# A fused block-sparse attention and feed-forward kernel: probabilities of the late pairs transposed by DMA, late scores two pairs at a time, orders dealt anew

## The chip, the cores and the metric

The kernel runs on one core of a Trainium2 chip. The metric is the device time of one execution in microseconds (us). The kernel before takes 307.81 us, the median of three runs (306.92 to 307.94).

A core has TensorE (PE in the profile; weight loads are shown apart as PEld), VectorE (DVE), ScalarE (ACT), GpSimd (POOL), SyncE (SP) and 16 DMA engines. Each engine takes its instructions in program order and waits on semaphores. Here SP does nothing but issue DMAs and load registers for them.

## The reference

The attention has 4 batches, 8 heads, 768 positions and a head size of 64. Positions form 24 blocks of 32. A query block sees its two neighbours and itself, the first and the last block, and three sampled blocks; the first and the last query block see everything. Behind it stands a feed-forward network (FFN) with 512 inputs, 2048 hidden units and 512 outputs over all 3072 tokens.

```python
scores = scale * np.matmul(q, k.transpose(0, 1, 3, 2))
mask = np.abs(blk_i - blk_j) <= window
mask = mask | (blk_i == 0) | (blk_j == 0) | (blk_i == n_blocks - 1) | (blk_j == n_blocks - 1)
...
mask[qb * block:(qb + 1) * block, kb * block:(kb + 1) * block] = True
scores = np.where(mask, scores, -1000000000.0)
scores = scores - np.max(scores, axis=-1, keepdims=True)
attn = np.exp(scores)
attn = attn / (np.sum(attn, axis=-1, keepdims=True) + 1e-09)
return np.matmul(attn, v).astype(np.float32)
...
h = x @ w_in
g = h * (1.0 / (1.0 + np.exp(-beta * h)))
return (g @ w_out).astype(np.float32)
```

## The kernel before

**Attention by pairs.** The 22 inner query blocks of a batch are taken two at a time: 11 pairs per batch, 44 in all, numbered n = 0 to 43. Pairs 33 to 43 are those of the last batch. The steps of a pair are:

- `kg`, `kn` (L635, L638): POOL copies the sampled blocks of K into the tile KG, POOL or DVE the neighbouring ones.
- `vv`, `vg` (L664, L720): SP loads block numbers into registers and issues the DMAs that gather the V blocks from a table in DRAM (VT) into VG. An ordinary late pair has seven: six of 32 KB for the sampled blocks, one of 192 KB for the neighbours. VG has four slots.
- `sc` (L759, L769): PE writes the masks of a pair (8 matmuls) and its scores (16 matmuls) in tiles of 64 x 32 into two PSUM banks.
- `mx`, `ex` (L782, L790): DVE takes the maxima, ACT the exponentials into the tile PP (three buffers).
- `nrm` (L813, pairs from 11 on): POOL or DVE multiplies PP by the reciprocal sums.
- `tp` (L827): PE transposes the 128 x 1024 probabilities in eight matmuls of 128 x 128 into a PSUM bank. `ptv` (L832, seen as L313 on DVE and L311 on ACT) copies that bank to PT (two buffers).
- `av` (L854 from pair 16 on, 16 matmuls; L862 before): PE multiplies PT by VG. `xv` copies the result to xT.

The first and last query blocks of a batch go another way (`gs` L917 to `gav` L971), with their own exponentials `ge` (L938), six transposes `gt` (L957) and copies.

**The FFN** goes over the tokens in eight groups G of 8 or 16 blocks, as soon as their attention stands in xT: `h` (L1033, 64 matmuls for a group, 128 x 256 or 128 x 512), `tanh` on ACT (L1039), `stt` on DVE (L1044), `y` (L1060, 128 x 512 matmuls), `oe` on ACT (L1070, seen as L317), `od` on SP (L1078, L1080, L1081) to the output. The last group needs the last pairs.

**The order.** Every step is a task with engines, a planned cost and a priority. `Plan.run` (L65) deals the tasks out in a planned time and fixes each engine's order; on the chip each engine then follows that order blindly. `OFFSET` (L53) shifts priorities by name, `YIELD` (L51) those of tasks that have just become ready. `plan = Plan(8, 6)` (L304) lets the FFN hold six of eight PSUM banks while attention is left. `GATES` (L259) names the pairs whose V loads the loads of w_in and w_out wait for, `QV` (L260) how many halves of V must be ready before each half of the first Q load.

Of the kernel before, what the change touches and what calls it, by code (L numbers as in the profile page):

```python
# [37 lines left out]
class Plan:  # L38
# [12 lines left out]
    YIELD = 10  # L51

    OFFSET = {'tp': 6.0, 'av': -5, 'gs': -1.0, 'gt': 5, 'gav': 10, 'trK': 2.1, 'nrm': 5, 'ex': -10, 'ptv': 9.1, 'xv': 1.4, 'oe': 20, 'gm': 2, 'ge': 10, 'pick': -10, 'tp1': 5, 'ptv1': 15, 'mx1': 0.5, 'tp2': -21.2, 'av2': -5, 'kn2': 30, 'ptv2': 5, 'tp3': 60, 'kn3': -5, 'ptv3': -15, 'hl3': 14.4, 'kg4': -15, 'ex4': 0.6, 'tp5': 1.3, 'av5': 60, 'kn5': -5, 'ptv5': 12.3, 'kg7': 5, 'mx7': -10.0, 'tp9': 5, 'xv9': 30, 'av10': 15, 'kn10': -15, 'av11': 15, 'kn11': 0.5, 'hl12': 5, 'sc13': -0.6, 'ex13': -3.7, 'av14': -1.3, 'tp15': -3.4, 'kn15': 4.3, 'mx0.0': 60, 'mx1.0': -5, 'ex2.1': -5, 'ex4.1': -15, 'ex5.0': 15, 'ex5.1': -60, 'mx7.0': 5, 'mx7.1': 30, 'win': -0.5, 'oe2': -1.2, 'y3': -6.6, 'h4': -1.0, 'stt4': 15, 'h5': -0.2, 'h7': 5}  # L53
# [164 lines left out]
def kernel(  # L218
# [11 lines left out]
    nc = tc.nc  # L230
# [28 lines left out]
    GATES = (2, 2, 5)  # L259
    QV = (1, 2)  # L260
    NLATE, PTA, ODS, AHEAD = 11, 1.0, 0.8, 3
    NHOT, NV = 0, 2
    NHL, UP = 4, 1024.0
    WIDE = 16
# [35 lines left out]
    osb = [sb(f"osb{i}", [P, D_MODEL], FP32) for i in range(NO)]  # L300
    VT = [dram.tile([S, D_MODEL], FP16, name=f"VT{b}") for b in range(B)]
    banks = [psum.tile([P, 512], FP32, name=f"bank{i}") for i in range(8)]

    plan = Plan(8, 6)  # L304
# [86 lines left out]
    for part, f in enumerate((emit_mask0, emit_mask1, emit_mask2)):  # L391
# [7 lines left out]
        deps=[t_mb], prio=-66, closes=("mask",))  # L399

# [127 lines left out]
    trK, trQ, evK, evQ, vperm, vtab = {}, {}, {}, {}, {}, {}  # L528
    later = {b: [] for b in range(B)}
    for b in range(B):  # L530
# [24 lines left out]
        for nm, s16, dstT, tr, ev in (("K", RK, KT, trK, evK), ("Q", RQ, QT, trQ, evQ)):  # L555
            for hp in range(NHP):
# [37 lines left out]
        else:  # L594
            vtab[b] = [add(f"vtab{b}", "SP", 0.4, lambda b=b, vt_rows=vt_rows: nc.sync.dma_start(
                out=vt_rows, in_=Vn[b % 2]), deps=vperm[b], prio=pr + 5, dma=1.9, slack=1.0, hw=1)]
# [14 lines left out]
    xlate, picks = [], []  # L611
    held_n, vv, vv_of, vg_last = {}, None, None, None
# [4 lines left out]
    for n, (b, p) in enumerate(order_pairs):  # L617
# [11 lines left out]
        def emit_kg(b=b, p=p, kt32=kt32, kg32=kg32):  # L629
            _, vals = nc.values_load_multi_w_load_instructions(  # L630
                offP[0:1, p, 0:6], engines=(ET.Pool,), min_val=0, max_val=(NB - 1) * W,
                skip_runtime_bounds_check_because="block numbers lie below the number of blocks")
            for g in range(2):
# [34 lines left out]
        if n >= NSEL and (p % NV == 0 or n == NSEL):  # L668
            held_n[n] = min(NV - p % NV, NPAIR - p)
# [3 lines left out]
        elif n < NSEL:  # L673
            vv = None
# [5 lines left out]
        def moves(n=n, vgb=vgb, vt=vt, vt8=vt8, i0=i0, first=head_v, w0=6 * (n - vv_of) if n >= NSEL else 0):  # L680
# [19 lines left out]
            elif i0 + 1 < NB - 2:  # L700
                yield 0.6, lambda v: (
                    vgb[0:3 * BLK, :, 1, :],
                    bass.AP(tensor=vt.tensor, offset=vt.offset + (i0 - 1) * BLK * D_MODEL,
                            ap=[[D_MODEL, 3 * BLK], [BLK * D_MODEL, 2], [1, D_MODEL]]))
            else:
                yield 0.3, lambda v: (vgb[0:3 * BLK, 0, 1, :], vt[(i0 - 1) * BLK:(i0 + 2) * BLK, :])
                yield 0.1, lambda v: (vgb[0:BLK, 1, 1, :], vt[(NB - 1) * BLK:NB * BLK, :])
                yield 0.2, lambda v: (vgb[BLK:3 * BLK, 1, 1, :], vt[i0 * BLK:(i0 + 2) * BLK, :])
            for g in range(2 if n >= NSEL else 0):
                for r in range(3):  # L710
                    yield RND, lambda v, g=g, r=r: (
# [3 lines left out]
        for k_, (cost, f) in enumerate(moves()):  # L715
            def emit_vg(vv_of=vv_of if n >= NSEL else None, f=f):
                o, i = f(held.get(vv_of))
                if i.dtype != U8:
                    o, i = o.bitcast(U8), i.bitcast(U8)
                nc.sync.dma_start(out=o, in_=i)  # L720
            vg[n].append(add(f"vg{n}.{k_}", "SP", 0.5, emit_vg,
                             deps=[vv] + vtab[b] + ([av[vlast(n)]] if vlast(n) >= 0 else []) +
                             ([ld["Q", 0, hp] for hp in range(NHP)] if NVG <= n < 2 * NVG else []),
                             prio=vprio(n, k_), dma=cost, hw=1))
# [29 lines left out]
        def emit_sc(n=n, b=b, p=p, i0=i0, kgb=kgb):  # L754
            bk = [bank(("S", n, u)) for u in range(2)]
            ns = 5 if p in (0, NPAIR - 1) else 3
            for hp in range(NHP):
                for u in range(2):
# [6 lines left out]
                        tile_position=(u * D, hp * BLK))  # L765
            for g in range(2):
                for hp in range(NHP):
# [7 lines left out]
        sc[n] = add(f"sc{n}", "PE", 0.31, emit_sc,  # L775
                    deps=[kg[n], kn[n], t_mask] + [evQ[b, hp] for hp in range(NHP)], prio=pr, lat=0.2,
                    opens=(("S", n, 0), ("S", n, 1)))
# [43 lines left out]
        def emit_tp(n=n, pb=pb):  # L821
            o = bank16(("T", n))
            for g in range(2):
                for c in range(2):
                    for u in range(2):
                        s = (g * 2 + c) * 2 + u
                        nc.tensor.transpose(out=o[:, s * P:(s + 1) * P],  # L827
                                            in_=pb[:, u, g, c * P:(c + 1) * P], identity=identity)
        tp[n] = add(f"tp{n}", "PE", 0.45, emit_tp, deps=[nrm[n]] if nrm[n] else [ex[n, 0], ex[n, 1]], prio=pr - 0.5, lat=0.2,
                    opens=(("T", n),))  # L830
        ptv[n] = add(f"ptv{n}", {"DVE": 0.61, "ACT": PTA}, None, lambda eng, n=n: copy_on(
            eng, PT[n % NPT], bank16(("T", n))),  # L832
            deps=[tp[n]] + ([av[n - NPT]] if n >= NPT else []), prio=pr - 0.5, closes=(("T", n),))
# [3 lines left out]
        def emit_av(n=n, vgb=vgb, wide=wide, late=late, hl=HL[n % NHL]):  # L837
            o = bank(("O", n))
            pt = PT[n % NPT].rearrange("x (g c u m) -> x g c u m", g=2, c=2, u=2)
# [66 lines left out]
    for b in range(B):  # L906
        for w, (blk, u) in enumerate((bl, u) for bl in (NB - 1, 0) for u in range(2)):
# [28 lines left out]
            def emit_ge(m=m, s_=s_, pg=pg):  # L936
                for hf in range(2):
                    nc.scalar.activation(  # L938
                        out=pg[:, hf * (S // 2):(hf + 1) * (S // 2)], in_=bank(("GS", m, hf))[:, 0:S // 2],
# [13 lines left out]
            def emit_gt(m=m, pg=pg):  # L953
                o = bank16(("GT", m))
                pj = pg[:, :].rearrange("x (p j) -> x j p", j=J)
                for j in range(J):
                    nc.tensor.transpose(out=o[:, j * P:(j + 1) * P], in_=pj[:, j, :], identity=identity)  # L957
            gt[m] = add(f"gt{m}", "PE", 0.34, emit_gt, deps=[gn[m]], prio=pr, lat=0.2, opens=(("GT", m),))
# [38 lines left out]
    for b in range(2, B):  # L997
        old = [x[n] for n, (bb, _) in enumerate(order_pairs) if bb == b - 2 for x in (kg, kn)] + gsc_all[b - 2]
        oldq = [sc[n] for n, (bb, _) in enumerate(order_pairs) if bb == b - 2] + gsc_all[b - 2]
        for hp in range(NHP):  # L1000
            trK[b, hp].deps += old
            trQ[b, hp].deps += oldq
# [12 lines left out]
    for G, sz in enumerate(sizes):  # L1015
# [38 lines left out]
        for s in range(sz // 4):  # L1054
# [21 lines left out]
            def emit_od(ob=ob, base=base, row=row):  # L1076
                if row + P <= S:
                    nc.sync.dma_start(out=out[base + row:base + row + P, :], in_=ob)  # L1078
                else:
                    nc.sync.dma_start(out=out[base + row:base + S, :], in_=ob[0:S - row, :])  # L1080
                    nc.sync.dma_start(out=out[base:base + row + P - S, :], in_=ob[S - row:P, :])  # L1081
            out_dma.append(add(f"od{G}.{s}", "SP", 0.9 if row + P > S else 0.45, emit_od, deps=[te],
                               prio=at(0.5 + 2.0 * s / sz), slack=ODS, dma=0.7, hw=2 if row + P > S else 1))
# [36 lines left out]
```

## Time and profile before

| | |
|---|---|
| median of three runs | 307.81 us |
| profiled execution | 306.43 us |
| its span in the trace | 304.6 us |
| granted TensorE clock, mean | 0.987 |
| ACT busy / exponentials L790 | 219.7 us / 81.5 us |
| FFN matmuls L1033 + L1060 | 93.8 + 92.3 us |
| POOL normalizing L813 | 63.5 us |
| DVE copying transposed probabilities | 39 of 44 pairs, 685 ns each |
| ACT doing the same | 5 of 44 pairs, 1015 ns each |

An engine's busy time is the time covered by its instructions; matmuls overlap in a pipeline, so the mean of one matmul (224 ns for a 128 x 128 transpose) is far more than what it adds. The chain of waits is followed back from the last instruction, at each step to what released it. There a row such as "0.45 PE bank L827 x8" says that eight instructions of line 827 took 0.45 us of the chain.

### The profile page before, as it was taken

The page shows a single profiled execution, that of the slowest core. Times are in us where ns is not written, and L with a number is a line of the kernel's source. Part 1 is how long each engine was busy: PE and PEld are TensorE (multiplying, and loading weights), DVE is VectorE, ACT ScalarE, POOL GpSimd, SP SyncE. Part 2 cuts the span into 40 slices and gives each one's busy share as a digit, 9 for nine tenths or more (in the row PEclk, how much of TensorE's full clock was granted, in tenths as well). Part 3 has the DMA queues.
Part 4 walks back from the last instruction along what each step waited for, and adds up shares of the span by engine and source line. Part 5 has one row for each costly group of instructions (what it writes and reads, how often), then busy time and mean ns, then how long its engine had stood idle before and what let it go on. Part 6 is the DMA issues. An engine that isn't in the chain of part 4 may idle for free.

```text
span 304.6 us, 11650 instructions
## 1 busy us (share of the span) xinstructions
PE 285.8 (94%) x4209; PEld 178.0 (58%) x4209; DVE 242.3 (80%) x562; ACT 219.7 (72%) x639; POOL 172.7 (57%) x513
## 2 busy tenths in 40 slices
PE   1699799999999999999998999999999999999994
PEld 0455678658855785655556555556555555554671
DVE  4758989999999999999999579989789765780260
ACT  3347579889797998898758599977689837771461
POOL 3069995044689588899784386868646942100000
PEclk9999969999999999999999999999999999999999
DMA  7999999977999362479933643244332232101202
GB/s 248 369 293 200 236 234 233 222 211 138 175 189 193 109 192 76 132 144 178 201 116 117 204 132 97 70 131 135 113 119 67 68 119 90 37 0 58 82 1 69
DMA packets 43443, 44.15 MB, mean 145 GB/s; under 512 B 6005, under 2 KB 39414, under 8 KB 43386
## 3 DMA queue, kind: packets, MB, share of 16 engines
q1 hardware_dynamic: 31056, 32.13, 35.0%
q0 software_dynamic: 12320, 11.27, 24.0%
q8 instruction: 33, 0.54, 0.7%
q14 instruction: 24, 0.20, 0.2%
q10 hardware_dynamic: 10, 0.01, 0.0%
HBM read 45.23 MB, written 9.44 MB: 179 GB/s over the span
## 4 chain that ended last, share of the span: by engine, by line
PE 69%; DVE 17%; DMA 9%; ACT 2%; issue 1%; SPq 0%; POOL 0%; DVEq 0%
PE bank L1033 25%; PE bank L1060 20%; PE bank L827 5%; DMA VG<-VT 4%; DVE ST L782 4%; PE bank L854 3%; PE bank L561 3%; DVE SG L931 3%; DVE VG L313 3%; DMA g<-in_k_dram 3%; PE bank L735 3%; DMA g<-VT 2%; PE bank L759 2%; PE bank L769 2%; PE bank L862 2%; DVE PTG L959 2%
## 5 line engine op out<-in xcount | busy, mean ns | idle before, releaser
L790 ACT ACTIVATE PP<-bank,ST 128x256 f16<-128x256 f32 x176 | 81.5, 478 | 22.7 <-DVE ST L782 13.6
L1033 PE MATMUL bank<-xT,w_in_sb 128*128 128x256 f16 (+1 forms) x512 | 93.8, 327 | 1.6 <-DVE g L1044 0.9
L1060 PE MATMUL bank<-w_out_sb,g 128*128 128x512 f16 x384 | 92.3, 380 | 0.0
L1044 DVE SCALAR_TENSOR_TENSOR g<-t,bank 128x512 f16<-128x512 f16 (+1 forms) x128 | 66.6, 546 | 19.4 <-ACT t L1039 19.0
L1039 ACT ACTIVATE t<-bank,beta_sb 128x512 f16<-128x512 f32 (+1 forms) x128 | 70.3, 593 | 12.4 <-PE bank L1033 8.4
L813 POOL TENSOR_SCALAR PP<-PP,ST 128x256 f16<-128x256 f16 x132 | 63.5, 499 | 27.6 <-DVE ST L807 27.0
L635 POOL COPY KG<-KT 128x64 f32 x264 | 51.8, 247 | 31.9 <-PE bank L769 18.9
L1033 PEld LDWEIGHTS <-w_in_sb 128*128 128x128 f16 x512 | 53.7, 114 | 26.1 <-issue 4.6
L782 DVE TENSOR_REDUCE ST<-bank 128x2 f32<-128x512 f32 x88 | 57.4, 681 | 3.4 <-PE bank L769 2.2
L1060 PEld LDWEIGHTS <-g 128*128 128x128 f16 x384 | 34.4, 98 | 38.2 <-issue 4.9
L790 ACT ACTIVATION_READ_ACCUMULATOR PP<-bank,ST 128x1 f32 x176 | 36.6, 208 | 0.0
L317 ACT ACTIVATE osb<-bank 128x512 f32<-128x512 f32 x24 | 14.5, 606 | 19.6 <-PE bank L1060 19.4
L313 DVE COPY PT<-bank 128x1024 f16<-128x1024 f16 x39 | 26.7, 685 | 2.4 <-PE bank L827 1.7
L827 PE MATMUL bank<-identity,PP 128*128 128x128 f16 x352 | 28.0, 224 | 0.3 <-ACT PP L790 0.3
L949 POOL TENSOR_SCALAR PG<-PG,SG 128x768 f16<-128x768 f16 x16 | 14.4, 902 | 23.8 <-ACT PG L938 19.8
L827 PEld LDWEIGHTS <-PP 128*128 128x128 f16 x352 | 22.7, 100 | 7.7 <-issue 1.6
L313 DVE CAST xT<-bank 64x256 f16<-64x256 f32 (+1 forms) x33 | 13.9, 420 | 8.4 <-ACT xT L311 7.4
L854 PEld LDWEIGHTS <-VG 128*128 128x128 f16 x448 | 16.5, 98 | 6.7 <-DMA VG<-VT 1.7
L313 POOL COPY KG<-KT 128x384 f32<-128x384 f32 (+3 forms) x47 | 19.6, 440 | 0.4 <-PE bank L769 0.4
L938 ACT ACTIVATE PG<-bank,SG 128x384 f16<-128x384 f32 x32 | 18.3, 585 | 2.1 <-DVE SG L933 1.9
L769 PE MATMUL bank<-KG,QT 64*32 64x256 f16 x704 | 18.5, 276 | 0.3 <-issue 0.3
L854 PE MATMUL bank<-PT,VG 128*128 128x64 f16 x448 | 17.7, 193 | 0.1
(107 smaller groups left out, 312.2 us busy)
## 6 DMA issues: line engine op xcount, KB each, us to landing
VG<-VT SPq DMA_DIRECT2D x220, 32.0 KB, 2.7
VG<-VT SPq DMA_DIRECT2D x32, 192.0 KB, 2.7
out_dram<-osb SPq DMA_DIRECT2D x20, 256.0 KB, 2.3
RV<-in_v_dram POOLq DMA_DIRECT2D x6, 384.0 KB, 6.6
RK<-in_k_dram POOLq DMA_DIRECT2D x6, 384.0 KB, 8.1
VT<-Vn SPq DMA_DIRECT2D x3, 768.0 KB, 3.9
RQ<-in_q_dram POOLq DMA_DIRECT2D x6, 384.0 KB, 6.5
w_in_sb<-in_moe_w_in_dram POOLq DMA_DIRECT2D x8, 256.0 KB, 8.2
```

Source lines behind the costliest of these rows:

```text
L313: (nc.vector if eng == "DVE" else nc.gpsimd).tensor_copy(out=out, in_=in_)
L635: nc.gpsimd.tensor_copy(out=kg32[:, g, :, (SR + r) * W:(SR + r + 1) * W], in_=kt32[:, :, bass.ds(vals[3 * g + r], W)])
L769: nc.tensor.matmul(bk[u][hp * BLK:(hp + 1) * BLK, g * 256:(g + 1) * 256], lhsT=QT[b % 2][u * D:(u + 1) * D, hp, (i0 + g) * BLK:(i0 + g + 1 ...
L782: mx[n, u] = add(f"mx{n}.{u}", "DVE", 0.6, lambda n=n, u=u, sb_=sb_: nc.vector.tensor_reduce(out=sb_[:, 0, 2 * u:2 * u + 2], in_=bank(("S" ...
L790: nc.scalar.activation(out=pb[:, u, g, :], in_=bank(("S", n, u))[:, g * 256:(g + 1) * 256], func=AF.Exp, bias=sb_[:, 0, 2 * u + g:2 * u + ...
L813: (nc.vector if eng == "DVE" else nc.gpsimd).tensor_scalar(out=pb[:, u, g, :], in0=pb[:, u, g, :], scalar1=sb_[:, 2, 2 * u + g:2 * u + g + ...
L827: nc.tensor.transpose(out=o[:, s * P:(s + 1) * P], in_=pb[:, u, g, c * P:(c + 1) * P], identity=identity)
L854: nc.tensor.matmul(o[:, (g * NHP + hp) * 2 * BLK:(g * NHP + hp + 1) * 2 * BLK], lhsT=vgb[:, g, c, hp * P:(hp + 1) * P], rhs=pt[:, g, c, :, ...
L1033: nc.tensor.matmul(o[:, 0:TW], lhsT=w_in_v[:, c, f // 4, f % 4, :], rhs=xT[:, c, c0:c0 + TW], start=(c == 0), stop=(c == NHP - 1))
L1039: lambda G=G, f=f, TW=TW, tt=tt: nc.scalar.activation(out=tt[:, 0:TW], in_=bank(("H", G, f))[:, 0:TW], func=AF.Tanh, bias=0.0, scale=beta_ ...
L1044: lambda G=G, f=f, TW=TW, tt=tt, gg=gg: nc.vector.scalar_tensor_tensor(out=gg[:, f, 0:TW], in0=tt[:, 0:TW], scalar=1.0, in1=bank(("H", G, ...
L1060: nc.tensor.matmul(o[:, :], lhsT=gg[:, f, s * P:(s + 1) * P], rhs=w_out_sb[:, f, :], start=(f == 0), stop=(f == N_FFC - 1))
```

## The change

- From pair 31 on (13 pairs) `tp` and `ptv` become one task `tpd` on SP: one DMA that transposes PP into PT. In the DMA it is 128 partitions x 8 blocks of 128.
- For that, and for all pairs, the eight blocks lie in PT in another order (`u g c` for `g c u`); `tp` and `av` follow it.
- In the last batch the scores of the pairs 34 and 35, 36 and 37, and so on to 42 and 43 become one task: both pairs' masks first, then both pairs' scores.
- `ge` reads its bank with a stride and writes PG in the order in which `gt` reads it, which is then contiguous.
- The last output tile is scaled in two halves, one on ACT and one on DVE, and its two DMAs are issued by SP and ACT.
- `OFFSET` is a new list, `YIELD` is 20 for 10, `Plan(8, 5)` for `Plan(8, 6)`, `GATES` (2, 2, 2) for (2, 2, 5), `QV` (0, 2) for (1, 2). Every engine's order is dealt anew by this.
- A table of row numbers (`rows96`) is built at the start: seven small POOL instructions, four small matmuls, one DVE copy. Nothing reads it: other ways of loading V and K that the new code holds are switched off (`IG`, `KD`, `GD`, `NBP`).

```diff
-    YIELD = 10
+    YIELD = 20
...
-    GATES = (2, 2, 5)
-    QV = (1, 2)
+    GATES = (2, 2, 2)
+    QV = (0, 2)
...
+    by_dma = lambda n: n >= TD[0] and n % TD[1] < TD[2]
+    TD = (31, 1, 1)
+
+    TWO, TWOP = 33, 1
...
-    plan = Plan(8, 6)
+    plan = Plan(8, 5)
...
+    t_rc = add("rowc", "POOL", 1.0, emit_rc, deps=[t_idx], prio=60)
...
+        two = [x for x in (n, n - 1) if TWO <= x and order_pairs[x][1] % 2 == TWOP and order_pairs[x][1] < NPAIR - 1]
+        sdeps = [kg[n], kn[n], t_mask] + [evQ[b, hp] for hp in range(NHP)]
+        if two == [n - 1]:
+
+            t = sc[n] = sc[n - 1]
+            t.deps += [d for d in sdeps if d not in t.deps]
+            t.opens += (("S", n, 0), ("S", n, 1))
+            halves[n - 1] += [emit_sm, emit_ss]
+        else:
+            halves[n] = [emit_sm, emit_ss]
+            sc[n] = add(f"sc{n}", "PE", 0.62 if two else 0.31, lambda h=halves[n]: [f() for f in h[0::2] + h[1::2]],
+                        deps=sdeps, prio=pr, lat=0.2, opens=(("S", n, 0), ("S", n, 1)))
...
+        if by_dma(n):
+            tp[n] = ptv[n] = add(f"tpd{n}", "SP", 1.38, lambda n=n, pb=pb: nc.sync.dma_start(
+                out=PT[n % NPT].rearrange("x (s m) -> x s m", m=P),
+                in_=pb[:, :, :, :].rearrange("x u g k -> x (u g k)"), transpose=True),
+                deps=[nrm[n]] + ptfree, prio=pr - 0.5, dma=0.3, hw=1)
...
-                        out=pg[:, hf * (S // 2):(hf + 1) * (S // 2)], in_=bank(("GS", m, hf))[:, 0:S // 2],
+                        out=pg[:, :].rearrange("x (j p) -> x j p", j=J)[:, :, hf * hw_:(hf + 1) * hw_],
+                        in_=bank(("GS", m, hf))[:, 0:S // 2].rearrange("x (p j) -> x j p", j=J),
...
+                te.emit, te.on = lambda ob=ob, G=G, s=s: scale_on(
+                    "ACT", ob[:, 0:256], bank(("Y", G, s))[:, 0:256], 0.5), {"ACT": 0.35}
+                tf = add(f"of{G}.{s}", "DVE", 0.35, lambda ob=ob, G=G, s=s: scale_on(
+                    "DVE", ob[:, 256:512], bank(("Y", G, s))[:, 256:512], 0.5), deps=list(te.deps), prio=te.prio,
+                    closes=(("Y", G, s),))
+                for q, en, r0, r1, d0 in ((nc.sync, "SP", 0, S - row, base + row), (nc.scalar, "ACT", S - row, P, base)):
+                    out_dma.append(add(f"od{G}.{s}{en}", en, 0.45, lambda q=q, ob=ob, r0=r0, r1=r1, d0=d0: q.dma_start(
+                        out=out[d0:d0 + r1 - r0, :], in_=ob[r0:r1, :]), deps=[te, tf], prio=te.prio, dma=0.4, hw=1))
```

More of the change, by code (lines that the diff above doesn't have):

```diff
@@ L300 @@
     osb = [sb(f"osb{i}", [P, D_MODEL], FP32) for i in range(NO)]
+    KQ = [dram.tile([NHP, S, P], FP16, name=f"KQ{i}") for i in range(2)]
     VT = [dram.tile([S, D_MODEL], FP16, name=f"VT{b}") for b in range(B)]
     banks = [psum.tile([P, 512], FP32, name=f"bank{i}") for i in range(8)]
-    plan = Plan(8, 6)
+    plan = Plan(8, 5)
     add = plan.add
@@ L399, with emit_rc, emit_rows @@
         deps=[t_mb], prio=-66, closes=("mask",))
+    NI = NB - 2
+    rows96 = sb("rows96", [3 * BLK, NI], I32)
+    cE = sb("cE", [1, 4, 3 * BLK])
+    sf16 = sb("sf16", [1, 3, NI])
+    mi96 = sb("mi96", [1, 3, BLK], I32)
+    def emit_rc():
+        V = nc.gpsimd
+        V.iota(mi96, pattern=[[0, 3], [1, BLK]], base=0, channel_multiplier=0, allow_small_or_imprecise_dtypes=True)
+        V.memset(cE[:, 0:3, :], 0.0)
+        for r_ in range(3):
+            V.memset(cE[:, r_, r_ * BLK:(r_ + 1) * BLK], float(BLK))
+        V.tensor_copy(out=cE[:, 3, :], in_=mi96[:, :, :].rearrange("o r m -> o (r m)"))
+        V.tensor_copy(out=sf16, in_=sf[:, :, :].rearrange("o a r -> o r a"))
+    t_rc = add("rowc", "POOL", 1.0, emit_rc, deps=[t_idx], prio=60)
+    def emit_rows():
+        o_ = bank("rows")[0:3 * BLK, 0:NI]
+        for r_ in range(3):
+            nc.tensor.matmul(o_, lhsT=cE[0:1, r_, :], rhs=sf16[0:1, r_, :], start=(r_ == 0), stop=False)
+        nc.tensor.matmul(o_, lhsT=cE[0:1, 3, :], rhs=ones[0:1, 0:NI], start=False, stop=True)
+    t_rows = add("rows", "PE", 0.2, emit_rows, deps=[t_rc, t_ident], prio=80, lat=0.2, opens=("rows",))
+    t_list = add("rowlist", "DVE", 0.1, lambda: nc.vector.tensor_copy(
+        out=rows96, in_=bank("rows")[0:3 * BLK, 0:NI]), deps=[t_rows], prio=80, closes=("rows",))
     SC = NSEL * 2 * 3 * BLK
@@ L555, with emit_pm @@
         for nm, s16, dstT, tr, ev in (("K", RK, KT, trK, evK), ("Q", RQ, QT, trQ, evQ)):
+            if b >= KD:
+                stage, tab = xT[:, :, b * S:(b + 1) * S], KQ[nm == "Q"]
+                pm = []
+                for hp in range(NHP):
+                    def emit_pm(eng, nm=nm, s16=s16, hp=hp, stage=stage):
+                        o = stage[:, hp, :].rearrange("p (j u d) -> p j u d", j=J, u=2)
+                        i = s16[:, 2 * hp:2 * hp + 2, :].rearrange("p u (j d) -> p j u d", j=J)
+                        if nm == "K":
+                            copy_on(eng, o, i)
+                        else:
+                            scale_on(eng, o, i, SCALE)
+                    pm.append(add(f"pm{nm}{b}.{hp}", {"DVE": 0.3, "ACT": 0.8}, None, emit_pm,
+                                  deps=[ld[nm, b, hp]] + ([tabK[b]] if nm == "Q" else []), prio=pr + hp))
+                    tr[b, hp] = pm[-1]
+                tb = add(f"tab{nm}{b}", TBE, 0.45 if TBE == "SP" else 0.8, lambda stage=stage, tab=tab: tq().dma_start(
+                    out=tab.rearrange("h (p j) m -> p h (j m)", j=J), in_=stage),
+                    deps=pm + ([tbT[nm, b - 1]] if (nm, b - 1) in tbT else []), prio=pr + 4, **tbk)
+                tbT[nm, b] = add(f"tt{nm}{b}", "SP", 3.8, lambda dstT=dstT, tab=tab, b=b: nc.sync.dma_start(
+                    out=dstT[b % 2][:, :, :].rearrange("x h s -> x (h s)"),
+                    in_=tab.rearrange("h s m -> (h s) m"), transpose=True),
+                    deps=[tb], prio=pr + 4, dma=0.5, hw=1)
+                if nm == "K":
+                    tabK[b] = tb
+                for hp in range(NHP):
+                    ev[b, hp] = tbT[nm, b]
+                continue
             for hp in range(NHP):
@@ L611 @@
     xlate, picks = [], []
+    held_k, halves = {}, {}
     held_n, vv, vv_of, vg_last = {}, None, None, None
@@ L672 @@
             vv_of = n
-        elif n < NSEL:
+        elif n < NSEL or n >= max(IG, 2 * NVG):
             vv = None
@@ L765, in emit_sc, with emit_ss @@
                         tile_position=(u * D, hp * BLK))
+        def emit_ss(n=n, b=b, i0=i0, kgb=kgb):
+            bk = [bank(("S", n, u)) for u in range(2)]
             for g in range(2):
```

130 lines of the change are left out of this document (86 added, 44 removed).

## The prediction

> **What bounds the kernel now.** I read the page's busy times and chain by engine first, then busy time by stage, then the chain row by row from 180 us on, then SP's timeline and the DMA issues.
>
> The page: engine totals, the chain's shares, and two groups (line, engine, operation, tiles, shape, count | busy us, mean ns | idle before).
>
> ```profile
> PE 285.8 (94%) x4209; PEld 178.0 (58%) x4209; DVE 242.3 (80%) x562; ACT 219.7 (72%) x639; POOL 172.7 (57%) x513
> ...
> PE 69%; DVE 17%; DMA 9%; ACT 2%; issue 1%; SPq 0%; POOL 0%; DVEq 0%
> ...
> L813 POOL TENSOR_SCALAR PP<-PP,ST 128x256 f16<-128x256 f16 x132 | 63.5, 499 | 27.6 <-DVE ST L807 27.0
> ...
> L827 PE MATMUL bank<-identity,PP 128*128 128x128 f16 x352 | 28.0, 224 | 0.3 <-ACT PP L790 0.3
> ```
>
> Busy time by stage (length, then PE, PEld, DVE, ACT, POOL, granted clock, DMA share, GB/s):
>
> ```profile
> 40.00:80.00 40.00, 38.88 (x746) 29.27 (x742) 37.72 (x111) 33.64 (x102) 19.02 (x53) 0.95 0.99 199
> ...
> 200.00:216.00 16.00, 15.50 (x251) 8.74 (x249) 15.36 (x40) 11.76 (x38) 10.91 (x27) 1.00 0.40 118
> 216.00:264.00 48.00, 48.00 (x597) 27.30 (x590) 35.29 (x68) 36.03 (x108) 27.07 (x82) 1.00 0.31 93
> 264.00:301.00 37.00, 36.60 (x209) 20.90 (x205) 14.86 (x29) 17.95 (x34) 0.00 (x0) 1.00 0.10 37
> ```
>
> PE is full from 216 us to the end, at full clock, with DMA engines at a third and DVE at three quarters. From 200 to 216 us DVE is full too (15.36 of 16). The chain there (start, us, what):
>
> ```profile
> 217.94 0.45 PE bank L827 x8
> 218.39 1.73 PE bank L1033 x8
> 220.11 0.47 PE bank L854 x16
> 220.58 0.87 PE bank L1033 x4
> 221.45 0.45 PE bank L827 x8
> 221.89 0.21 PE bank L759 x8
> 222.10 0.22 PE bank L769 x16
> 222.32 0.98 PE bank L1033 x4
> ...
> 294.56 6.06 PE bank L1060 x28
> 300.62 0.02 issue
> 300.64 0.60 ACT osb L317
> ```
>
> PE's rows follow each other without a gap. So what leaves PE in this stage leaves the path, as long as PE doesn't begin to wait. One pair's eight transposes are 0.45 us there. Four FFN matmuls take 0.87 us, but 0.98 right behind scores: going from tiles of 64 x 32 to whole ones costs 0.11.
>
> **The change, part by part.**
>
> 1. *Transposes off PE.* 13 pairs x 0.45 us = 5.8 us. All lie on the gapless PE chain or in the stretch just before it (pair 31 is transposed at 196 us). I count all of it.
>
> 2. *Scores of two pairs.* Five of the pairs' changes of tile size go: 5 x 0.11 = 0.55 us.
>
> 3. *Copies off DVE.* 13 copies of 685 ns. After 216 us DVE has room (35.3 of 48), so nothing. In the stretch where DVE ends the chain (199.6 to 215.2 us) two of them lie, pairs 32 and 33: 0 to 1.4 us, since PE was 97% busy there and its FFN work must be done in any case. I take the middle, 0.7.
>
> 4. *The end.* ACT's 0.60 us for the last tile becomes two halves; DVE's 128 x 256 scaling out of a bank (line 319) had a mean of 416 ns, ACT's 393, so about 0.2 less. SP's second issue no longer stands behind the first (start, us):
>
> ```profile
> 217.88 2.23 SPq L720 DMA_DIRECT2D VG<-VT  x5
> ...
> 301.26 0.33 SPq L1080 DMA_DIRECT2D out_dram<-osb  x1
> 301.65 0.42 SPq L1081 DMA_DIRECT2D out_dram<-osb  x1
> ```
>
> The last issue began 0.39 us after the first. Together 0.6 us.
>
> 5. *What the transposing DMA costs.* No row has one. The nearest, with size and median us from issue to landing:
>
> ```profile
> VG<-VT SPq DMA_DIRECT2D x220, 32.0 KB, 2.7
> VG<-VT SPq DMA_DIRECT2D x32, 192.0 KB, 2.7
> out_dram<-osb SPq DMA_DIRECT2D x20, 256.0 KB, 2.3
> ```
>
> PP is also 256 KB. *SP's time x for one.* Low end: an ordinary issue, 0.42 us whatever the size. High end: eight issues, one for each 128 x 128 block, 3.4 us. It is one instruction but has eight blocks to describe, so I take the geometric middle, 1.2. *Room on SP:* SP's order in the changed kernel has, from the transposition of pair 31 to that of pair 40, 57 ordinary issues and 4 register loads. At 0.47 us a step (five in 2.23 us and the gap to the next) and 0.8 (loads took 0.73 to 1.02 us in the trace) that is 30 us. On PE's order, priced with the steps above, `av` of pair 31 and of pair 40 are 46.3 us apart. For nine transpositions 16.3 us are left: x up to 1.8 us is hidden. Behind pair 40 stand 13.8 us of FFN matmuls in one block, so SP is not pressed there.
>
> *Latency.* A transposition waits on SP for POOL's normalization. Behind it on SP wait the next pairs' V loads and an output store; PE's `av` waits for both. In the trace of before, scores to the end of the normalization took 4.9 to 8.6 us for pairs 31 to 43, mean 6.2. Landing: 2.3 us as the store, plus 1.2 - 0.4 for the longer issue: 3.1. So 9.3 us, at worst 11.7; the second pair of a double score has another pair's exponentials ahead (1.9 us in the trace): 11.2, at worst 13.6. PE's new order leaves between a pair's scores and its `av` 12.4, 12.1, 11.1 us (pairs 31 to 33), then 10.8 and 12.1 (34, 35), 11.4 and 15.3, 11.4 and 16.2, 13.1 and more. The mean fits everywhere; the worst is late by 1.0 (pair 34) and 1.5 (pair 35). A late pair also holds up SP's queue for those behind it. From 0 to 4 us of waiting, I take 1.0.
>
> DMA engines: 13 x 256 KB more, at a share of 0.31 and 93 GB/s; two copies of the load of this stage would still be under the 0.99 seen from 40 to 80 us. Nothing.
>
> 6. *The rest.* Pairs 0 to 30 keep all their PE work; their orders alone differ. PE's idle time between 20 and 216 us is 6 us in sum, so re-dealing can win at most that and could lose as much; I see no reason for either sign and take 0. The first Q load goes ahead of the first V table store; V loads wait for both stores, and the second is behind a V cast as before: 0. w_out's loads no longer wait for pair 5's V loads; they stand in POOL's queue behind the same loads of w_in: 0, up to 2.7 us (what the table's 384 KB V loads into the tile g took longer to land than the 32 KB ones, 8.4 against 5.7, in the stage of 20 to 40 us). The dead table: about 1 us of POOL at 3.6 us, where POOL is idle until K's transposes at 15.5; 0. `ge` with a stride: ACT copies KT out of a bank with a stride at 825 ns for 768 elements, 1.07 ns each, against 606 ns for 512, 1.18 each: 0.
>
> Sum: -5.8 - 0.55 - 0.7 - 0.6 + 1.0 = -6.65 us. The profiled execution took 306.43 us (span 304.6), which would become 299.8. That execution lies 1.4 us under the median of the runs; from the median, 307.81 - 6.65 = **301.2 us**.
>
> **The rivals.**
>
> *S: SP becomes the bound (slower).* If x is over 1.8 us, the nine transpositions from pair 32 to 40 push each other, the V loads behind them, and `av`. The gain is gone at x = 1.8 + 6.65 / 9 = 2.5 us. At 3.4 us it costs 9 x 1.6 = 14.4: 315.6 us. For it: one instruction describes eight blocks, and SP is already in use for 30 of 46 us. Against: an issue's price does not grow with bytes (0.33 to 0.42 us from 32 to 256 KB). 0.13.
>
> *P: blocks are transposed one after another.* If each block had a landing of its own, 2.3 us x 8 = 18.4 us would stand in place of 5.1 us, the mean distance of two `av` on the new order; 9 x 13.3 = 120 us more, 421 us. Against it: six separate 32 KB loads of one pair overlap in the trace. 0.04. The Trainium skill (VectorE: DVE Perf Modes, The three transpose paths, and its rules for kernel authors) speaks for it: it gives 390 ns for a 128 x 128 transpose on TensorE and 1309 ns by DMA, and says to use TensorE where a PSUM destination is acceptable. By its figure eight in a row would be an estimated 10.5 us and the result some 9 x 5.4 = 48 us slower. The chain's 0.45 us for eight shows that here PE pays 56 ns each in a row, not 390; no run yet shows the 1309.
>
> *R: the new orders of pairs 0 to 30 decide.* They may win up to the 6 us of idle: 295 to 299, chance 0.14, under 295 0.03. Or a load comes late for one engine and all that is blindly queued behind it: up to 6 us lost and more, 309 to 312, 0.07. For it: DMA is at 0.99 from 40 to 80 us, where any later load shows.
>
> *W: `av` waits for most transpositions*, at the worst latencies: 4 to 5.5 us of the gain go, 304 to 307. 0.07.
>
> *N: no difference*, within 0.3% (about what a measurement of this kernel can tell from no change): x near 2.5, 0.06.
>
> **How the numbers follow.** Forecast (299 to 304): 0.46. Faster by over 0.3%: 0.46 + 0.14 + 0.03 + 0.07 = 0.70; within 0.3%: 0.06; slower: 0.13 + 0.04 + 0.07 = 0.24. Range 295 to 311: it leaves out 0.03 below and above it most of S, P, and the upper end of R, some 0.15.
>
> **What would show it.** Right: 248 PE transposes in the group of 352; DVE's copies of PT fewer by about 13; SP's transposing instruction under 1.8 us and its landing near 3; from pair 31 on PE full, with no waits of `av` on a DMA that writes PT; the last store's issue beside SP's. Wrong: SP's rows back to back with long transpositions (S), landings over 5 us (P), idle PE before `av` (W), or a PE that reaches pair 31's scores at another time than the 190 us of before by more than 2 us (R).

## The result and the profile after

| | before | after |
|---|---|---|
| median | 307.76 us (6 runs, 306.92 to 309.16) | 304.26 us (6 runs, 300.53 to 305.11) |
| ratio after / before | | 0.9857 (95%: 0.9818 to 0.9895) |
| profiled execution, its span | 306.43, 304.6 us | 304.74, 302.9 us |
| last matmul's end to the span's end | 4.0 us | 4.6 us |

The change makes the kernel 1.4% faster, 4.4 us by the ratio (3.2 to 5.6). Forecast were 6.65 us, for 301.2; 304.26 us lies just above the forecast's 299 to 304 us, where rival W's range begins. A second set of six runs of the same kernel gave 302.77 (301.23 to 305.64), inside the forecast, with ratio 0.9853; its profiled execution took 301.81 us, and it is called *after, again* below.

The page of after: engine totals, the chain's shares, two groups.

```profile
PE 279.5 (92%) x4109; PEld 173.8 (57%) x4109; DVE 237.5 (78%) x556; ACT 218.6 (72%) x641; POOL 170.0 (56%) x513
...
PE 49%; DVE 23%; issue 7%; ACT 6%; POOL 6%; DMA 5%; POOLq 2%; SPq 0%; DVEq 0%; ACTq 0%
```

```profile
L929 PE MATMUL bank<-identity,PP 128*128 128x128 f16 x248 | 20.4, 225 | 1.2 <-ACT KT L328 0.6 <-POOL PP L915 0.3 <-DVE g L1166 0.3
...
L963 PE MATMUL bank<-PT,VG 128*128 128x64 f16 x448 | 17.5, 193 | 2.2 <-DMA PT<-PP 1.5 <-ACT osb L334 0.6 <-ACT PP L892 0.2
```

The transposes fell from 352 to 248 matmuls and PE from 285.8 to 279.5 us. New is what ended the idle time ahead of the `av` matmuls (now L963): 1.5 us of DMAs that write PT. The profile infers the releaser's name; by the times all five of these waits, 2.2 us, ended 0.04 to 0.24 us after a transposition had landed. The same by stage, after (length, then PE, PEld, DVE, ACT, POOL, granted clock, DMA share, GB/s):

```profile
216.00:264.00 48.00, 46.31 (x529) 24.42 (x528) 33.84 (x65) 36.53 (x103) 26.35 (x76) 1.00 0.53 136
```

PE was full from 216 to 264 us before, 48.00 of 48. Now it stands idle for 1.7 us, while no other compute engine is full. SP's timeline shows who is (start, us, instruction, count):

```profile
223.18 5.24 SPq L810 DMA_DIRECT2D VG<-VT  x9
228.53 1.24 SPq L933 DMA_TRANSPOSE PT<-PP  x1
229.86 1.91 SPq L810 DMA_DIRECT2D VG<-VT  x4
232.70 1.25 SPq L933 DMA_TRANSPOSE PT<-PP  x1
234.00 4.52 SPq L810 DMA_DIRECT2D VG<-VT  x7
```

From one row to the next there is no gap but for register loads. From the transposition of pair 31 to that of pair 40 SP stands idle for 0.3 us of 48.9 (*after, again*: 0.7 of 48.4). In *after, again* a transposition begins 0.03 to 0.83 us after its normalization has ended in pairs 31 to 35, but 2.7, 2.8, 1.9, 2.1 and 4.3 us after it in pairs 36 to 40: the probabilities are ready, and SP is still issuing V loads.

**A ledger.** To compare stages of kernels whose PE work differs, I price each matmul at the step it adds on a gapless chain (0.056 us for a transpose, 0.216 for 128 x 512, and so on, from the rows of before) and take the elapsed time less the priced work up to there. That difference is what PE has lost so far. In us:

| kernel | PE work in all | lost at 200 us | at 220 | at 260 | at 280 |
|---|---|---|---|---|---|
| before | 275.3 | 24.3 | 25.2 | 25.2 | 25.3 |
| after | 269.3 | 26.2 | 26.8 | 28.9 | 28.9 |
| after, again | 269.3 | 23.9 | 23.8 | 26.1 | 25.9 |

The work fell by 6.0 us, as forecast. The table also shows why the two executions of after differ by 3 us: 2.3 of them are there by 200 us. By their ledgers at 100 and 120 us (21.0 and 24.0 us lost; again: 20.6 and 22.0) most of it arises at one place, told at the end. The rest of this text uses *after, again* for the stage from 200 us on.

### The profile page after: what moved, and what is told of

Read it like the earlier page. It is cut to its first block, busy times and chain, and to the rows that moved or that the text cites. A ratio compares the mean times of both kernels' runs of the same rounds, so it can differ in the third digit from the quotient of the medians.

```text
span 302.9 us, 11451 instructions
## 1 busy us (share of the span) xinstructions
PE 279.5 (92%) x4109; PEld 173.8 (57%) x4109; DVE 237.5 (78%) x556; ACT 218.6 (72%) x641; POOL 170.0 (56%) x513
## 2 busy tenths in 40 slices
DMA packets 57170, 47.55 MB, mean 157 GB/s; under 512 B 19733, under 2 KB 53142, under 8 KB 57114
## 4 chain that ended last, share of the span: by engine, by line
PE 49%; DVE 23%; issue 7%; ACT 6%; POOL 6%; DMA 5%; POOLq 2%; SPq 0%; DVEq 0%; ACTq 0%
PE bank L1155 17%; PE bank L1182 14%; DVE ST L884 5%; PE bank L825 4%; DVE g L1166 4%; PE bank L929 3%; POOL KG L710 3%; DMA g<-in_k_dram 3%; DVE SG L1040 3%; POOL PP L915 2%; PE bank L963 2%; PE bank L971 2%; ACT PP L892 2%; PE bank L632 2%; ACT t L1161 2%
## 5 line engine op out<-in xcount | busy, mean ns | idle before, releaser
L1166 DVE SCALAR_TENSOR_TENSOR g<-t,bank 128x512 f16<-128x512 f16 (+1 forms) x128 | 67.0, 547 | 16.3 <-ACT t L1161 15.8
L710 POOL COPY KG<-KT 128x64 f32 x264 | 52.4, 249 | 25.6 <-PE bank L862 10.5
L892 ACT ACTIVATION_READ_ACCUMULATOR PP<-bank,ST 128x1 f32 x176 | 37.4, 212 | 0.0
L1061 POOL TENSOR_SCALAR PG<-PG,SG 128x768 f16<-128x768 f16 x13 | 13.1, 1010 | 24.4 <-ACT PG L1049 15.2
L334 ACT ACTIVATE osb<-bank 128x512 f32<-128x512 f32 (+1 forms) x24 | 14.2, 590 | 16.1 <-PE bank L1182 16.0
L330 DVE COPY PT<-bank 128x1024 f16<-128x1024 f16 x30 | 20.4, 683 | 3.8 <-PE bank L929 3.6
L330 DVE CAST xT<-bank 64x256 f16<-64x256 f32 (+1 forms) x35 | 14.6, 418 | 9.9 <-PE bank L963 6.8
L929 PE MATMUL bank<-identity,PP 128*128 128x128 f16 x248 | 20.4, 225 | 1.2 <-ACT KT L328 0.6
L963 PEld LDWEIGHTS <-VG 128*128 128x128 f16 x448 | 16.1, 98 | 9.2 <-issue 4.3
L929 PEld LDWEIGHTS <-PP 128*128 128x128 f16 x248 | 16.2, 101 | 6.0 <-issue 1.1
L963 PE MATMUL bank<-PT,VG 128*128 128x64 f16 x448 | 17.5, 193 | 2.2 <-DMA PT<-PP 1.5
L330 POOL COPY KG<-KT 128x384 f32<-128x384 f32 (+3 forms) x43 | 16.6, 411 | 1.3 <-PE bank L862 1.3
L328 ACT CAST xT<-bank 64x256 f16<-64x256 f32 (+1 forms) x30 | 11.3, 375 | 8.2 <-PE bank L1089 3.9
```

The lines of the kernel that those rows point to most:

```text
L330: (nc.vector if eng == "DVE" else nc.gpsimd).tensor_copy(out=out, in_=in_)
L892: nc.scalar.activation(out=pb[:, u, g, :], in_=bank(("S", n, u))[:, g * 256:(g + 1) * 256], func=AF.Exp, bias=sb_[:, 0, 2 * u + g:2 * u + ...
L929: nc.tensor.transpose(out=o[:, s * P:(s + 1) * P], in_=pb[:, u, g, c * P:(c + 1) * P], identity=identity)
L963: nc.tensor.matmul(o[:, (g * NHP + hp) * 2 * BLK:(g * NHP + hp + 1) * 2 * BLK], lhsT=vgb[:, g, c, hp * P:(hp + 1) * P], rhs=pt[:, g, c, :, ...
L1166: lambda G=G, f=f, TW=TW, tt=tt, gg=gg: nc.vector.scalar_tensor_tensor(out=gg[:, f, 0:TW], in0=tt[:, 0:TW], scalar=1.0, in1=bank(("H", G, ...
```

## The experiments

All were timed in five rounds beside the kernel before. "By the ratio" gives the gain from the ratio, at 307.7 us.

**PE transposes.** The changed kernel, with the DMA switched off.

```diff
-    TD = (31, 1, 1)
+    TD = (99, 1, 1)
```

> The changed kernel with all transposes on PE (bound 31 set to 99); its orders are the same up to pair 31. Theory (the DMA transposes are what gains, 5.8 us of PE work less about 1.8 us of waiting): 4 us slower than the changed kernel, about 308. Rival (the waiting eats the gain, and the new orders and double scores are what is left): within 1 us of the changed kernel.

306.20 us, ratio 0.9965 (0.9943 to 0.9988). All of the change but the transposing DMA is worth 1.1 us (0.4 to 1.8); the DMA adds 3.4 of the 5.8 us that it takes from PE, with the orders behind pair 31 dealt anew for it. The ledger of this run: 22.8 lost at 200 us, 23.2 at 260, so +0.4 in the stage where *after, again* has +2.2.

**A transposition in four pieces.** Each as four DMAs of two blocks; the orders of the other engines stay.

```diff
+                for c in range(0, 8, 2):
+                    nc.sync.dma_start(out=o[:, c:c + 2, :], in_=i[:, c * P:(c + 2) * P], transpose=True)
```

> The changed kernel with each transposition issued as four DMAs of two blocks; PE's, DVE's, ACT's and POOL's orders are the same. One transposition should take SP about 4 x 0.5 = 2.0 to 2.4 us in place of 1.25. Theory (SP already runs about 2 us behind the normalizations of pairs 36 to 39, so every us on SP counts): 9 x 1.0 = 6 to 10 us slower, about 312. Rival (POOL's normalization is what is late, and SP has room up to 1.8 us): 0 to 4 us slower.

352.71 us, ratio 1.1429 (1.1382 to 1.1477). I had expected some microseconds. SP's timeline of this kernel:

```profile
208.97 5.06 SPq L937 DMA_TRANSPOSE PT<-PP  x4
214.13 0.98 SPq L810 DMA_DIRECT2D VG<-VT  x2
```

and PE's longest waits:

```profile
PE bank L966 <- DMA PT<-PP: 33.4, 21, 5.6
```

A DMA of a quarter of the size takes SP the same 1.2 us. Four take 5.06, which is 3.8 more than one; 13 x 3.8 = 49 us, and the kernel lost 49.9. From the transposition of pair 31 to that of pair 40 it took 82.6 us in place of 48.4, 34.1 more, while the transpositions there took 32.7 us more of SP's time. So on the average of these 3.8 us each microsecond added to SP's work on a pair came back in full: with one DMA for each pair SP has next to no slack, where the prediction had left 0.6 us a pair.

**Fewer V loads.** The changed kernel leaves out three of SP's row loads for each pair from 33 on; the orders of the other four engines are the same instruction for instruction.

```diff
-                    yield RND, lambda v, g=g, r=r: (
+                    yield RND, lambda v, g=g, r=r: None if n >= 33 and g == 1 else (
```

> The changed kernel, with the three row loads of VG for the second query group left out in pairs 33 to 43 (VG keeps an earlier pair's rows there): 33 of SP's issues fewer, the orders of PE, DVE, ACT and POOL are those of the changed kernel. Theory SP (the transposing DMAs are late because SP's queue is full with V loads): SP saves 1.4 us a pair, the transposition is issued at once after the normalization in pairs 36 to 40 too, and the 1.5 to 2 us that the changed kernel loses after pair 31 against the version with PE transposes come back: 301 us, 1.5 to 2 faster than the changed kernel. Rival POOL (the normalization itself is late, SP's queue hardly matters): within 0.5 us of the changed kernel. Rival end (the loss lies behind the last pair, in the experts and the stores): no change either.

299.85 us (298.34 to 300.65), ratio 0.9753 (0.9732 to 0.9774): 3.1 us faster than the changed kernel by the two ratios. Its stage row and SP's timeline:

```profile
216.00:264.00 48.00, 47.95 (x480) 25.93 (x479) 35.34 (x67) 39.26 (x105) 23.17 (x70) 1.00 0.53 123
```

```profile
227.19 1.99 SPq L812 DMA_DIRECT2D VG<-VT  x4
231.55 1.25 SPq L935 DMA_TRANSPOSE PT<-PP  x1
232.86 1.99 SPq L812 DMA_DIRECT2D VG<-VT  x4
```

PE is full again, 47.95 of 48, and has no wait on a DMA from 200 to 262 us. SP now stands idle for 0.3 to 2.4 us ahead of the transpositions of pairs 31 to 39, and each begins 0.03 us after its normalization has ended; in *after, again* the probabilities waited for SP. Ledger: 22.8 lost at 200 us, 22.6 at 260. The normalization ends as late behind the scores as in *after, again* (a mean of 8.4 us in pairs 31 to 39 against 8.6), and it doesn't matter. This is the clearest run for SP's queue. Landing took 2.8 us at the median in both (means 3.0 and 2.9), and the DMA share of the stage is 0.53 in both, so a lighter load on the DMA engines isn't what won.

**Normalization on DVE.** From pair 34 on, away from POOL.

```diff
-            nrm[n] = add(f"nrm{n}", {"POOL": 1.85, "DVE": 0.8}, None, emit_nrm, deps=[rc], prio=pr - 0.5)
+            on_dve = n >= 34
+            nrm[n] = add(f"nrm{n}", "DVE" if on_dve else {"POOL": 1.85, "DVE": 0.8}, 0.8 if on_dve else None,
+                         (lambda f=emit_nrm: f("DVE")) if on_dve else emit_nrm, deps=[rc], prio=pr - 0.5)
```

> The changed kernel, with the normalization of pairs 34 to 43 on DVE (0.8 us a pair) in place of POOL (1.85), so that it ends some 1 us earlier, while DVE gets 8 us more work. Theory SP: the transposition still waits for its place in SP's queue, so the time changes by less than 1 us either way. Rival POOL: the transposition starts 1 to 3 us earlier in each pair and 1.5 to 2 us come back, 301 us.

302.32 us, ratio 0.9831 (0.9792 to 0.9870): no difference to the changed kernel that the runs can tell. Lost from 200 to 260 us: 23.9 to 25.8, much as before the edit. SP is as full as in the changed kernel, idle for 0.3 us of 47.5 from the transposition of pair 31 to that of pair 40. This speaks for the theory of SP, though not cleanly: the scheduler planned with the shorter cost and put some `av` nearer to its scores (pair 38: 8.7 us of PE work between them in place of 11.8).

**Before, with the DMA alone.** The kernel before, with transposition by DMA from pair 31 on and PT's new layout, nothing else.

```diff
+    by_dma = lambda n: n >= 31
...
+        if by_dma(n):
+            tp[n] = ptv[n] = add(f"tpd{n}", "SP", 1.38, lambda n=n, pb=pb: nc.sync.dma_start(
```

> The kernel before with one part of the change: pairs from 31 on are transposed by DMA from SP, with PT laid out in the order of the blocks; nothing else of the change. The PE work taken away is 5.8 us. If the transposing DMA alone makes the gain and SP's queue costs 2 us of it: 303.5 to 304.5 us. If the other parts (orders dealt anew) are needed for it to fit, SP's queue and the av matmuls wait more here: 305 to 308.

307.80 us, ratio 0.9986 (0.9963 to 1.0009): no gain, and my first figure was 4 us off. PE's waits from 200 to 262 us:

```profile
PE bank L862 <- DMA VG<-VT: 1.7, 1, 1.7
PE bank L862 <- ACT PP L791: 0.8, 1, 0.8
PE bank L965 <- POOL PG L957: 0.8, 1, 0.8
PE bank L862 <- DMA PT<-PP: 0.7, 2, 0.5
```

The names mislead: the wait of 1.7, the first of 0.8 and the two of 0.7 us in sum ended 0.04 to 0.14 us after a transposition had landed (pairs 37, 36, 31 and 40; those of 37 and 40 took 4.8 and 4.2 us to land). The work is 269.5 us, as little as after, but 26.4 lost at 200 us grow to 32.0 at 280: 5.6 us, which is all of the gain. One thing that differs is the room in PE's order. The priced PE work that stands between a pair's scores and its `av`, in pairs 31 to 40:

| kernel | least | median | most |
|---|---|---|---|
| before | 7.7 | 9.8 | 11.7 |
| before with the DMA alone | 9.3 | 10.7 | 12.6 |
| after | 11.1 | 12.2 | 16.3 |

The measured path is, in *after, again*, 8.4 us from the scores' end to the normalization's end, 1.6 of waiting for SP and 3.4 from the start of the issue to `av` (means of pairs 31 to 40), 13.4 in all. The orders dealt anew leave 12.8 on average, the old ones with the DMA 10.7. The other thing is SP, which is full in both: from the transposition of pair 31 to that of pair 40 it needs 49.2 us here (61 ordinary issues), with 46.0 us of PE work between the same two `av`, against 48.4 (57 issues) and 46.3 in *after, again*. The runs don't separate the two.

**After, dealt as before.** All of after's work, with the offsets, gates and bank settings of before.

```diff
-    YIELD = 20
+    YIELD = 10
...
-    GATES = (2, 2, 2)
-    QV = (0, 2)
+    GATES = (2, 2, 5)
+    QV = (1, 2)
...
-    plan = Plan(8, 5)
+    plan = Plan(8, 6)
```

(and the old `OFFSET`.)

> The changed kernel with the offsets, gates and the planner's settings of the kernel before: the work is that of the changed kernel, the orders are dealt as before. If the orders are worth nothing (the prediction's value): 302.5 to 304. If they are fitted to the DMA transposes and make room for them on SP: 305 or more, no better than the version with PE transposes (306.2).

309.25 us, ratio 1.0056 (1.0031 to 1.0081). The orders are needed, but this run doesn't say that the transposing DMA is why: 29.8 us are lost by 200 us, 5.9 more than in *after, again*, and only 3.4 from there to 280. Most of the loss lies ahead of the transposing DMAs; why the old offsets fit the changed list of steps so badly there stays open.

**V loads from ACT's queue.** The neighbour loads of the pairs from 33 on, issued by ACT in place of SP.

```diff
-            eng = "POOL" if (n >= max(NBP, 2 * NVG) and where) or where == 3 else "SP"
+            eng = "ACT" if n >= 33 and where == 1 else "SP"
```

> The changed kernel, with those loads of VG that need no register (one a pair, of three neighbour blocks of both groups; three in one pair) issued from ACT's queue in pairs 33 to 43, in place of SP's. All work is done. Theory SP: SP saves 0.47 us a pair, 5 to 6 us in all, about a third of what leaving out three loads a pair saved, so some 0.7 to 1.5 of the 3.1 us come back: 301.4 to 302.2 us. Rival: ACT pays 0.4 us for each issue in a stretch where it feeds the exponentials, and the time stays at 302.5 to 304.

307.06 us (304.44 to 311.52), ratio 0.9953 (0.9920 to 0.9985): 3 us slower than the changed kernel. Neither side had foreseen that much. ACT's timeline and PE's waits from 200 to 262 us:

```profile
226.05 0.72 ACT L1161 ACTIVATE t<-bank,beta_sb 128x512 f16<-128x512 f32 x1
226.49 0.33 ACTq L810 DMA_DIRECT2D VG<-VT  x1
226.62 0.73 ACT L1161 ACTIVATE t<-bank,beta_sb 128x512 f16<-128x512 f32 x1
226.92 0.41 ACTq L810 DMA_DIRECT2D VG<-VT  x1
```

```profile
PE bank L963 <- DMA VG<-VT: 2.6, 1, 2.6
PE bank L963 <- ACT PP L892: 2.4, 2, 1.3
```

The issues themselves are cheap, 0.33 and 0.41 us, and overlap the activations. The names of PE's waits mislead again: the three waits of these rows ended 0.09 to 0.24 us after a transposition had landed (pairs 31, 33 and 36). Pair 36's, issued at 226.42 us, took 5.1 us to land. Three of the 13 transpositions had a load from ACT issued less than 0.7 us behind them, those of pairs 36, 40 and 41, and just these landed after 4.8 to 5.1 us; the others took 2.8 to 4.2. So the likelier reason is that the loads on a second queue run beside the transposition and delay it; no run tests this alone, and the orders behind pair 33 were dealt anew here too. ACT then waits for PE (3.2 us for a bank of the FFN), and its next load stands behind that. Lost from 200 to 260 us: 22.6 to 29.9.

**The end as before**, and **the last tile whole** (ACT scales it in one piece, the stores stay on two queues).

```diff
-            if G == len(sizes) - 1 and s == sz // 4 - 1 and row + P > S:
+            if False:
```

> The changed kernel with the end of the kernel before: the last output tile is scaled whole by ACT and both of its stores go from SP. The trace of the changed kernel has 4.3 to 4.6 us between the last matmul and the end, that of before 4.0. If that is the end's own cost: 0.3 to 0.6 us faster than the changed kernel, 302.3 to 302.6. By the prediction's step 4 it would be 0.6 us slower, 303.5.

> The changed kernel with the last tile scaled whole by ACT; the two stores stay on two queues. Theory (the halves run one after the other, 0.38 + 0.42 us and a gap): 0.2 us faster, the last store's issue 0.62 us behind the last matmul in place of 0.83. Rival (halves overlap, and the profile showed an accident): 0.2 us slower.

302.16 us, ratio 0.9811 (0.9769 to 0.9854), and 302.73, ratio 0.9840 (0.9815 to 0.9864): neither can be told from the changed kernel by its time. The traces tell them apart: from the last matmul's end to the span's end 4.3 us with the old end (4.0 to 4.3 in the four traces that have it), 4.4 with the whole tile, 4.6 in both executions with the change's end (4.4 to 4.7 in all nine traces).

**Scores one pair at a time.**

```diff
-    TWO, TWOP = 33, 1
+    TWO, TWOP = 99, 1
```

> The changed kernel with the scores of each pair computed by themselves, as before, and the orders that the scheduler deals for that. By the prediction's step 2, 0.5 us slower than the changed kernel, 303.4 us. If two pairs at a time cost time, since the second pair's banks are held longer: faster than the changed kernel. If the new order of the late steps matters, up to 2 us slower.

303.38 us, ratio 0.9851 (0.9810 to 0.9891), the same as the changed kernel. The ledger has 269.9 us of PE work, 0.6 more, as step 2 counted. The order of the late pairs changed with it, so this run neither confirms the gain in time nor refutes it.

**An attempt at a better one.** Gathers from POOL in place of six loads from SP, from pair 36 on; normalization on DVE; the end as before.

```diff
-    IG, IGT = 99, 1.28
+    IG, IGT = 36, 1.28
```

(and the edits of *normalization on DVE* and *the end as before*.)

> The changed kernel with three edits, all work done: the row loads of VG for pairs 36 to 43 come as two gathers a pair (one of 96 rows for each group) from POOL, in place of six loads with register addresses from SP; the normalization of pairs 34 to 43 runs on DVE, which makes the room on POOL; the end is that of the kernel before. Theory SP: SP has 2.8 us a pair less to issue in pairs 36 to 43, twice what leaving out three loads took away, the transpositions start right behind their normalization, and the 3.1 us of that experiment come back, or 2 of them, since pairs 33 to 35 keep their loads: 299.5 to 301 us. Rival: a gather from POOL lands late (other loads from POOL's queue took a median of 6.2 to 8.8 us from issue to landing, those from SP 2.6) or stretches DVE's work beside it, and the av matmuls wait for VG in place of PT: 303 us or more.

303.04 us, ratio 0.9833 (0.9804 to 0.9862): no better than the changed kernel. The named rival isn't the reason: the gathers took POOL 0.95 us each and landed after 3.2. The transpositions of pairs 36 to 40 do begin 0.03 us behind their normalization, and SP stands idle for 17 us between those of pairs 31 and 40. But the orders were dealt anew for the shorter planned path and left 9.9, 12.0, 8.7, 11.5 and 10.0 us of PE work between scores and `av` there, against 11.8, 15.5, 11.8, 16.3 and 13.5. The path itself took 9.8, 13.3, 10.5, 13.7 and 11.2. PE's waits from 200 to 262 us:

```profile
PE bank L965 <- DMA PT<-PP: 2.6, 2, 1.5
```

What SP's relief won was given back (22.8 to 26.7 lost). The transpositions also landed later, after 3.3 us in the mean and up to 4.9, against 3.0, so the tighter order isn't shown to be the only reason. Whether the same relief on the changed kernel's own PE order would reach the 299.85 us of the run with fewer loads stays open. Of the kernels that do all the work none is measurably faster than the changed kernel.

## Why the prediction was right, and where it was off

- **Step 1, transposes off PE: right.** 248 are left, and the work fell by 6.0 us (steps 1 and 2: 6.35).
- **Step 2, double scores: right in work** (0.6 us), not resolved in time.
- **Step 3, copies off DVE: fits.** From 200 to 220 us *PE transposes* lost 0.9 us, *after* 0.6, *after, again* and *fewer V loads* about nothing; the step had 0.7. No run changed these copies alone.
- **Step 4, the end: wrong in sign.** In the trace of after the halves don't run side by side:

```profile
298.33 0.38 ACT L334 ACTIVATE osb<-bank 128x256 f32<-128x256 f32 x1 [2.86 <-PE bank L1182]
298.74 0.42 DVE L336 TENSOR_SCALAR osb<-bank 128x256 f32<-128x256 f32 x1 [6.39 <-ACT osb L334]
299.20 0.33 SPq L1206 DMA_DIRECT2D out_dram<-osb  x1
299.20 0.38 ACTq L1206 DMA_DIRECT2D out_dram<-osb  x1
```

DVE's half is released by ACT's half of the same tile, and starts 0.41 us behind it in all nine traces with this end, so both take 0.87 us up to the issue where one piece took 0.62. And the span ends 3.7 us after two issues at once, while it ended 3.0 us (before; 3.2 in three other kernels) after the second of two in a row: the 0.4 us of the issue order came back behind the issues. In place of -0.6 stands +0.4 to +0.6.

- **Step 5, the transposing DMA: its size nearly right, its room and its waiting wrong.** One takes SP 1.26 us at the median (taken: 1.2), and lands after 2.8 at the median, 3.0 in the mean (taken: 3.1). By the Trainium skill (VectorE: DVE Perf Modes, The three transpose paths) a 128 x 128 transpose by DMA takes 1309 ns; eight blocks in one DMA landed here after 2.8 us, so that figure doesn't add up over blocks, and rival P with it falls. The row of DMA issues of after:

```profile
PT<-PP SPq DMA_TRANSPOSE x13, 2.8
```

  Three terms failed. The time from scores to the normalization's end was taken from before, 6.2 us; on the new orders it was 8.4. "Room on SP: x up to 1.8 us is hidden" priced SP's ordinary work at 30 us. In *after, again* the same 57 issues and 4 register loads took 34.2: an issue with the gap behind it took 0.53 us in the mean, where the prediction had 0.47 from five quick ones (0.54 in the trace of before from 198 to 262 us). Of the 46.3 us of PE work that leaves 12.1, or 1.35 for each of nine transpositions, and they took 1.51 each with their gaps, two of them 2.0. So SP's work came to 47.8 us beside 46.3 of PE's, and SP was the longer one. Nor is it even: a pair's transposition stands behind four to nine V loads that SP begins when a VG slot comes free, 2.1 to 5.4 us in a row. The wait of 1.6 us for SP, in the mean, was no term of the sum. In place of 1.0 us *after, again* lost 2.1 to 2.2 from 200 us on.

  The prediction's list of late pairs is too short by its own numbers: its worst of 11.7 us is late by 0.9 us in pair 34, not 1.0, and also late in pairs 33, 36 and 38, by 0.6, 0.3 and 0.3. In *after, again* PE waited ahead of `av` in pairs 35, 36 and 39.

- **Step 6, the rest: near in its sum by luck, wrong in its reason.** All but the DMA is worth 1.1 us with the end's loss in it. But orders and DMA don't add: with the old orders the DMA wins 0.4 us (-0.3 to 1.1), with the new ones 3.4. I had priced the orders for pairs 0 to 30 and read the room for the late ones off the new order, without asking what the old order would have left.

The sum, on the spans of before and *after, again* (304.6 to 300.0): -6.0 of work, +0.6 lost up to 280 us, +0.1 from there to the last matmul and +0.6 behind it, which makes -4.7; measured -4.6. The 0.6 up to 280 us is -0.4 up to 200 us, -1.0 to 220 and +2.0 behind it. So of the 2.2 us that the gain fell short, some 1.2 are the waiting of step 5 and some 1.2 the end; the sign and the main term held. Of the rivals, S and W both came true in small: SP is full from pair 31 on, though x stayed under the 1.8 us that S asked for, and some `av` wait, 2 us in sum, not 4 to 14. R didn't: by 200 us the orders had won 0.4 us in one execution and lost 1.9 in the other.

## What to carry to other kernels

Price the room on a queue with the mean step of a long stretch, not with its quickest rows: 0.06 us more for each of 57 issues, and register loads a little longer, took 4.2 of the 16.3 us counted here. And room in the sum isn't yet room at the moment: an instruction that must go out at a given moment waits for all that its engine has begun before it, so ask what stands just ahead of it in the order, and for how long. A longer but cheaper path (a DMA for matmuls and a copy) pays only if the order leaves that much other work between its two ends; measure the path on the new order, not the old. And every fix that moves instructions lets a scheduler close the gap that it opened, so hold the other engines' orders still when one queue is to be tested.

## What the runs showed of the hardware

- **A transposing DMA took SP about 1.2 us at both sizes tried**: 1.2 us with two blocks of 128 x 128, and with eight 1.23 to 1.37 us in 11 of 13, against a median of 0.37 us for other issues. The other two of the 13 took 1.8 to 2.8 us; why isn't shown. Cutting it up costs in full, as the run of four pieces shows. Packets under 512 B rose from 6005 to 19733 and are 6005 again in *PE transposes*, so each of the 13 brings 1056 small packets.
- **It usually landed 2.7 to 2.9 us after its issue, but now and then after up to 5.1**, and most of PE's waiting for `av` in both executions of after stands behind such late ones: in *after, again* pairs 36 and 39 landed after 3.3 and 3.6 us, and PE waited 0.64 us for each.
- **One DVE copy took five times its usual time beside POOL.** In after's profiled execution, a row of DVE, then POOL's row at the same time:

```profile
103.08 2.67 DVE L330 COPY Vn<-RV 128x1536 f16<-128x1536 f16 x1
```

```profile
103.28 1.83 POOL L915 TENSOR_SCALAR PP<-PP,ST 128x256 f16<-128x256 f16 x4
```

  In *after, again* the same copy, 0.4 us ahead of POOL's normalization, took 0.85. In the nine other kernels that keep this stretch's order it took 0.8 us seven times and 2.5 us twice (four pieces, normalization on DVE). The Trainium skill (SBUF — State Buffer, SBUF: two separate sides) says that the two engines share a port pair which a GpSimd instruction or a DVE instruction of some modes holds alone, the other waiting; the row fits that, but no run here tests it. Most of the difference between the two executions arises in the 20 us around this copy, 1.6 of 2.3 us; that the copy is the reason is likely and not shown.
- **The span ended no sooner after two stores at once than after two in a row**: 3.5 to 3.8 us after two issues at the same moment on two queues, 3.4 to 3.6 us after the first of two that SP began 0.39 us apart.
